# A four-layer transformer block on one core: the MLP's input rows transposed by VectorE instead of TensorE, with an exchange of quarters through DRAM

## The chip, the cores and the metric

The kernel runs on one core of a Trainium2 chip. The metric is the device time of one execution in microseconds; the median of the runs is what counts. Profiles come from one execution, and times in them run from the start of its span.

## The reference

Two attention layers and two MLP layers alternate on x of shape 1 x 2048 x 640 in float32. Both attention layers share their weights, and so do both MLPs.

```python
x = A_x
x = x + _A_ref(_layernorm(x), A_wqkv, A_wo)             # 32 heads of 20, softmax
x = x + _B_ref(_layernorm(x), B_w1, B_b1, B_w2, B_b2)   # 640 -> 1536, relu squared, 1536 -> 640
x = x + _A_ref(_layernorm(x), A_wqkv, A_wo)
x = x + _B_ref(_layernorm(x), B_w1, B_b1, B_w2, B_b2)

def _B_ref(x, w1, b1, w2, b2):
    h = jnp.einsum("bsd,df->bsf", x, w1) + b1
    r = jnp.where(h > 0, h, 0)
    return jnp.einsum("bsf,fd->bsd", r * r, w2) + b2
```

## The kernel before, in words

Rows are handled in blocks of 512 (`QB`), four to a layer (`NQB`), each of four row tiles of 128 x 640. Matrix products are made of three: every operand is split into a high part in a shorter float format (`hi`, fp32r) and the rest (`lo`), and hi x lo, lo x hi and hi x hi are accumulated (`THREE`). The split operands of the MLP are `xnT` (five tiles of 128 x 2 x 512, the normalised rows with features on the partitions) and `h`.

A layer runs `qkv`, `attention`, and then the part around the change:

- `add_heads(qb, ...)` multiplies the heads by `wo`: for each of four row tiles two chains of 15 matmuls, each followed by an add on VectorE into the row tile `x` and one call of `side()`; then the tile is stored to DRAM (`d_x`). It runs for all four blocks, one after the other. After each of the first three blocks four tiles of `w1` (512 KB each) are loaded, after the last one the remaining three and then all sixteen tiles of `w2` (480 KB each): nineteen loads in a row.
- `mlp(qb, ...)` runs for the four blocks: six chains of 15 matmuls with `w1` (one for each f; ScalarE makes relu, VectorE squares it, ScalarE makes the high part of h and VectorE the low part, in this order for each f), then eight chains of 18 matmuls with `w2`, each followed by an add on VectorE into the residual row; then the same again for the second half of F. After f = 1 to 4 of the first half the block's residual rows are loaded from `d_x` and GpSimd adds the bias `b2`. `side()` is called after each f and each w2 chain.

`side()` pops one entry from a list `steps`. That list is how the work for the next block gets its place in each engine's order: each engine executes its instructions, and SP issues its transfers, in the order in which the Python code calls them. Transfers on SP carry one of eight completion semaphores in turn; a transfer is issued only after the one eight places earlier has landed. `xtile` takes from a pool of eleven 128 x 640 tiles (`NX`), in which row tiles, residual rows and the relu results `r` share space; `slot` takes from 42 larger ones.

Before the change, `normal_rows` (a generator of nine steps) loads the next block's four row tiles, takes their statistics on VectorE (`stats`, with the inverse root on GpSimd), and normalises them on VectorE. In `mlp` its first step comes at the seventh `side()`, after the first w2 chain. Then `transposed` makes twenty 128 x 128 transposes on TensorE into five PSUM banks, and ScalarE and VectorE split each bank into high and low part over 512 columns. It is called once before the first block of the MLP, and inside blocks 0 to 2 after the third w2 chain of the second half (`(1, 0, 2)`).

Of the kernel before, what the change touches and what calls it, by code (L numbers as in the profile page):

```python
# [8 lines left out]
F32 = mybir.dt.float32  # L9
F32R = mybir.dt.float32r  # L10
AF = mybir.ActivationFunctionType
ALU = mybir.AluOpType
# [4 lines left out]
P = 128  # L17
S = 2048
D = 640
# [3 lines left out]
KD = D // P  # L23
NF = F // P
QB = 512
NQB = S // QB
# [13 lines left out]
def tile_layers(  # L40
# [11 lines left out]
    nc = tc.nc  # L52
# [6 lines left out]
    dram = ctx.enter_context(tc.tile_pool(name="dram", bufs=1, space=DRAM))  # L59
# [3 lines left out]
    def name(p):  # L63
        n_alloc[0] += 1
        return f"{p}{n_alloc[0]}"

    def slot(shape, dtype, label):
        return arena.tile(shape, dtype, tag="slot", name=name(label))

    def dma(eng, dst, src):  # L70

        if dst.dtype == F32R:
            dst = dst.bitcast(F32)
        if src.dtype == F32R:
            src = src.bitcast(F32)
        eng.dma_start(dst, src)

    def xtile(label):
        return xpool.tile([P, D], F32, tag="x", name=name(label))
# [30 lines left out]
    ps_all = Ring(0, 1, 2, 3, 4, 5, 6, 7)  # L110

    ident = cpool.tile([P, P], F32, name="ident")
# [105 lines left out]
    def at_2(f, hw, hf):  # L218

        return (((f // 6) * 2 + hf) * 6 + f % 6) * 2 + hw  # L220
# [26 lines left out]
    d_m = dram.tile([2, P, 2, 32], F32R, name="d_m")  # L247
    d_s = dram.tile([NBLK, 4, QB], F32, name="d_s")
    d_r = dram.tile([NBLK, 4, QB], F32, name="d_r")
    d_x = [dram.tile([S, D], F32, name=f"d_x{i}") for i in range(3)]  # L250

    def stats(x):

        st = small.tile([P, 2, 6], F32, tag="bst", bufs=3, name=name("bst"))
        mv = small.tile([P, 2], F32, tag="mv", bufs=6, name=name("mv"))
        for i in range(2):
            nc.vector.bn_stats(st[:, i, :], x[:, i * HALF : (i + 1) * HALF])  # L257
        nc.vector.bn_aggr(mv, st)
        var = mv[:, 1:2]
        nc.gpsimd.tensor_tensor(var, var, eps_t, op=ALU.add)  # L260
        nc.gpsimd.tensor_tensor(var, var, half_t, op=ALU.pow)
        return mv

    def normalise(eng, x, mv):
        eng.tensor_scalar(x, x, mv[:, 0:1], mv[:, 1:2], op0=ALU.subtract, op1=ALU.mult)  # L265

    def split_to(dst_hi, dst_lo, src):

        nc.scalar.copy(dst_hi, src)  # L269
        nc.vector.tensor_sub(dst_lo, src, dst_hi.bitcast(F32))  # L270

    def split_on_pool(dst_hi, dst_lo, src, r=None):

        if r is None:
            r = xtile("r")[:, :QB]
        nc.scalar.copy(r, src)
        pool_hi(dst_hi, r)
        pool_lo(dst_lo, r, dst_hi.bitcast(F32))
# [3 lines left out]

    def pool_lo(dst, a, b):
        nc.gpsimd.tensor_sub(dst, a, b)  # L284

    THREE = ((0, 0), (0, 1), (1, 0))

    def row_tile(src, r):
        t = xtile("x")
        dma(nc.sync, t, src[r * P : (r + 1) * P, :])  # L290
        return t
# [4 lines left out]
    def chain(dst, pairs):  # L296
        last = len(pairs) - 1
        for n, (a, b) in enumerate(pairs):
            nc.tensor.matmul(dst, a, b, start=(n == 0), stop=(n == last))  # L299
# [732 lines left out]
    def heads(q, qb, k):  # L1032

        ot = slot([P, 2, QB], F32R, "ot")
        dma(q, ot.rearrange("p l t -> p (l t)"), d_o[k * P : (k + 1) * P, qb])
        ready.setdefault(qb, {})[k] = ot
# [17 lines left out]
                side()  # L1054
            dma(nc.sync, x_mid[(qb * 4 + i) * P : (qb * 4 + i + 1) * P, :], x)

    def normal_rows(qb, x_src, res):

        xs = [row_tile(x_src, qb * 4 + i) for i in range(4)]
        yield  # L1060
        mvs = []
        for x in xs:
            mvs.append(stats(x))
            yield
        for x, mv in zip(xs, mvs):
            normalise(nc.vector, x, mv)
            yield
        res.extend(xs)

    def transposed(xs):  # L1070
        xnt = []
        for k in range(KD):
            dst = ps_all("xt")
            for i in range(4):
                nc.tensor.transpose(  # L1075
                    dst[:, i * P : (i + 1) * P], xs[i][:, k * P : (k + 1) * P], ident
                )
            t = slot([P, 2, QB], F32R, "xnT")
            split_to(t[:, 0, :], t[:, 1, :], dst)
            xnt.append(t)  # L1080
        return xnt

    def mlp(qb, xnt, x_mid, x_dst, side, nxt):

        xs, res = [], None
        for fh in range(2):
            hs = []
            for f in range(fh * 6, fh * 6 + 6):
                dst = ps_all("pu")
                chain(dst, [  # L1090
                    (w_1.piece(f * 10 + hw * KD + k), xnt[k][:, hx, :])
                    for k in range(KD)
                    for hw, hx in THREE
                ])
                if qb == NQB - 1:
                    w_1.past(f * 10 + 9)
                r = xtile("r")[:, :QB]
                nc.scalar.activation(r, dst, AF.Relu, bias=b1_t[:, f : f + 1])  # L1098
                nc.vector.tensor_mul(r, r, r)  # L1099
                h = slot([P, 2, QB], F32R, "h")  # L1100
                split_to(h[:, 0, :], h[:, 1, :], r)
                hs.append(h)
                if fh == 0 and f in (1, 2, 3, 4):
                    x = row_tile(x_mid, qb * 4 + f - 1)
                    nc.gpsimd.tensor_add(x, x, b2_t)
                    xs.append(x)
                side()
            for hf in range(2):
                c = slice(hf * HALF, (hf + 1) * HALF)
                for i in range(4):  # L1110
                    dst = ps_all("y")
                    chain(dst[:, :HALF], [
                        (hs[f % 6][:, hx, i * P : (i + 1) * P], w_2.piece(at_2(f, hw, hf)))
                        for f in range(fh * 6, fh * 6 + 6)
                        for hx, hw in THREE
                    ])
                    x = xs[i]
                    nc.vector.tensor_add(x[:, c], dst[:, :HALF], x[:, c])  # L1118
                    if fh == 1 and hf == 1:
                        r0 = (qb * 4 + i) * P  # L1120
                        dma(nc.sync, x_dst[r0 : r0 + P, :], x)
                    side()
                    if (fh, hf, i) == (1, 0, 2) and nxt:
                        res = transposed(nxt)
            if fh == 0 and qb == NQB - 1:
                w_2.past(at_2(5, 1, 1))
        return res

    def layer(first, x_a, x_m, x_e, front_0, ahead):
        qkv(first, x_a, front_0)  # L1130
        if first:
            dma(nc.sync, b1_t, b1.rearrange("(f p) -> p f", p=P))
            dma(nc.sync, b2_t, b2.partition_broadcast(P))
        xs = []
        attention(first, x_a, xs)
        steps = []
        for i in sorted(split):
            steps += [split.pop(i), None]
        steps += [lambda: heads(nc.scalar, NQB - 1, KD - 1)]
        for k in range(KD - 1):  # L1140
            heads(nc.sync, NQB - 1, k)

        def side():
            if steps:
                (steps.pop(0) or (lambda: None))()

        def all_steps():
            while steps:
                side()

        for qb in range(NQB):
            if qb + 1 == NQB:
                rows = []
                norm = normal_rows(0, x_m, rows)
                steps.extend([lambda: next(norm, None)] * 10)
            add_heads(qb, x_a, x_m, xs, side)
            for s in range(qb * 4, min(qb * 4 + 4, w_1.n)):
                w_1.load(s)
            if qb > 1:
                all_steps()  # L1160
        w_o.drop()
        xnt = transposed(rows)
        for s in range(w_2.n):
            w_2.load(s)
        for qb in range(NQB):
            rows = []
            if qb + 1 < NQB:
                norm = normal_rows(qb + 1, x_m, rows)
                steps.extend([None] * 6 + [lambda norm=norm: next(norm, None)] * 10)
            elif ahead:  # L1170
                some = lambda: [next(ahead, None) for _ in range(2)]
                steps.extend([None] * 7 + [some] * 21)
            xnt = mlp(qb, xnt, x_m, x_e, side, rows if qb + 1 < NQB else None)
            if qb + 1 < NQB:
                all_steps()
        steps.clear()
        w_1.drop()
        w_2.drop()
# [33 lines left out]
    for h in range(4):  # L1212
        r = 32 * h + DH
# [32 lines left out]
```

## Time and profile before

| | before |
|---|---|
| median of 3 runs | 3727.01 us (3724.64 to 3731.82) |
| profiled execution | 3726.99 us, span 3724.3 us |
| mean granted TensorE clock | 0.996 |
| TensorE matmuls | 3684.9 us busy (99%), 23572 |
| VectorE, ScalarE, GpSimd busy | 2790.1, 2553.6, 829.2 us |
| transposes at L1075 | 160, 19.9 us busy |

PE is TensorE's matmuls and PEld its weight loads, DVE is VectorE, ACT is ScalarE, POOL is GpSimd, SPq the queue from which most transfers are issued. In a timeline a row gives the start, the length, the engine, the line, the operation, output and input tiles with their shapes, the count of merged instructions, and in brackets how long the engine stood idle before it and what ended that. In a group's row the numbers behind the bar are busy time and mean duration in ns of one instruction.

### The profile page before, as it was taken

To read this page: it belongs to the slowest core of one execution; us is meant where nothing else is said; L and a number is where in the kernel's file an instruction comes from. 1 tells how busy PE (TensorE), PEld (TensorE's weight loads), DVE (VectorE), ACT (ScalarE), POOL (GpSimd) and SP (SyncE) were. 2 spreads that over 40 slices of the span, in tenths; PEclk is the share of its full clock that TensorE was granted. 3 is DMA by queue.
4 is the path that set the end of the run, shared out by engine and by line. 5 is a ranking of instruction groups with operands and counts; after the bars stand their busy time and mean duration, and the time that the engine had idled before them with its cause. 6 is when DMAs were issued, how large, how long until landed. Compare 5 with 4: busy or idle time off the path is not lost.

```text
span 3724.3 us, 64225 instructions
## 1 busy us (share of the span) xinstructions
PE 3684.9 (99%) x23572; PEld 2111.4 (57%) x23572; DVE 2790.1 (75%) x4796; ACT 2553.6 (69%) x4888; POOL 829.2 (22%) x921
## 2 busy tenths in 40 slices
PE   7999999999999999999999999999999999999999
PEld 5677343433444336999876763434434334368998
DVE  7788999999999992444567889999999999814443
ACT  2454999999999995122224459999999999941211
POOL 6430234322112211111153201121121121201110
PEclk9999999999999999999999999999999999999999
DMA  7564454432211125511255533222222111364111
GB/s 230 183 211 139 121 165 144 133 108 74 59 53 51 45 89 194 228 43 43 96 194 174 176 122 87 70 73 56 75 76 57 46 49 49 103 215 189 43 47 39
DMA packets 257682, 404.88 MB, mean 109 GB/s; under 512 B 67708, under 2 KB 114556, under 8 KB 257368
## 3 DMA queue, kind: packets, MB, share of 16 engines
q1 hardware_dynamic: 256824, 399.08, 34.1%
q8 instruction: 186, 3.05, 0.3%
q10 hardware_dynamic: 544, 1.71, 0.2%
q14 instruction: 128, 1.05, 0.1%
HBM read 263.84 MB, written 136.81 MB: 108 GB/s over the span
## 4 chain that ended last, share of the span: by engine, by line
PE 95%; DVE 3%; ACT 1%; DMA 1%; POOL 0%; issue 0%; SPq 0%; ACTq 0%; DVEq 0%; POOLq 0%
PE banks L604 27%; PE banks L299 20%; PE banks L592 20%; PE banks L495 16%; PE banks L310 7%; PE banks L357 4%; DVE mx L516 1%; PE banks L1075 0%; PE banks L387 0%; DVE bst L257 0%; DVE h L270 0%; DVE r L1099 0%; ACT h L269 0%; DVE x L265 0%; ACT r L1098 0%
## 5 line engine op out<-in xcount | busy, mean ns | idle before, releaser
L599 ACT ACTIVATE e<-banks 128x512 f32<-128x512 f32 x4096 | 2114.3, 604 | 64.0 <-PE banks L592 4.7
L507 DVE TENSOR_REDUCE mx<-banks 128x1 f32<-128x512 f32 x2940 | 1845.9, 683 | 189.9 <-PE banks L495 116.3
L495 PE MATMUL banks<-k,q 60*128 60x512 f32 x3744 | 1155.7, 436 | 6.3 <-DVE mx L516 2.3
L592 PE MATMUL banks<-q,k 62*128 62x512 f32 x4096 | 1152.7, 435 | 2.1 <-DVE mx L516 1.7
L604 PE MATMUL banks<-e,vg 128*32 128x512 f32 x8192 | 1093.8, 605 | 0.0
L592 PEld LDWEIGHTS banks<-q,k 62*128 62x128 f32 x4096 | 601.1, 185 | 701.1 <-ACT e L599 665.9
L495 PEld LDWEIGHTS banks<-k,q 60*128 60x128 f32 x3744 | 538.1, 185 | 332.1 <-DVE mx L507 206.0
L604 PEld LDWEIGHTS banks<-e,vg 128*32 128x32 f32 x8192 | 161.6, 108 | 357.9 <-issue 330.9
L527 ACT ACTIVATE rl<-banks 128x512 f32<-128x512 f32 x352 | 191.3, 596 | 248.0 <-PE banks L495 247.9
L299 PE MATMUL banks<-w,h 128*128 128x320 f32 x2304 | 351.1, 311 | 2.7 <-DVE h L270 2.5
L299 PEld LDWEIGHTS banks<-w,h 128*128 128x128 f32 x2304 | 339.4, 188 | 11.7 <-DVE h L270 6.4
L299 PE MATMUL banks<-xnT,w 128*128 128x512 f32 x1440 | 331.6, 391 | 0.0
L310 PE MATMUL banks<-xnT,wqk 128*128 128x512 f32 x1200 | 320.5, 410 | 3.7 <-POOL wqk L284 2.5
L537 DVE CUSTOM_DVE_ANT_0 rl<-banks,rl 128x512 f32<-128x512 f32 x352 | 229.1, 688 | 112.3 <-PE banks L495 103.3
L1098 ACT ACTIVATE r<-banks,b_t 128x512 f32<-128x512 f32 x96 | 66.1, 688 | 356.3 <-PE banks L299 352.5
L299 PEld LDWEIGHTS banks<-xnT,w 128*128 128x128 f32 x1440 | 270.7, 189 | 55.7
L516 DVE TENSOR_REDUCE mx<-banks 128x2 f32<-128x1024 f32 x226 | 271.7, 1220 | 16.1 <-PE banks L495 15.1
L310 PEld LDWEIGHTS banks<-xnT,wqk 128*128 128x128 f32 x1200 | 217.8, 191 | 88.3 <-issue 42.7
L648 POOL TENSOR_TENSOR few<-few,minus_t 128x16 f32<-128x16 f32 x62 | 179.8, 2900 | 286.1 <-DMA few<-d_s 285.9
L659 POOL TENSOR_TENSOR o<-o 128x512 f32<-128x512 f32 x62 | 79.5, 1283 | 612.7 <-DMA o<-d_r 376.9
L1118 DVE TENSOR_TENSOR x<-banks,x 128x320 f32<-128x320 f32 x128 | 62.9, 491 | 196.2 <-PE banks L299 187.0
L281 POOL CAST mr<-nt 128x32 fp32r<-128x32 f32 x64 | 13.4, 210 | 808.6 <-DVE nt L563 775.1
(76 smaller groups left out, 1986.6 us busy)
## 6 DMA issues: line engine op xcount, KB each, us to landing
q<-d_qk SPq DMA_DIRECT2D x744, 80.0 KB
d_qk<-ev SPq DMA_DIRECT2D x80, 512.0 KB
k<-d_qk SPq DMA_DIRECT2D x468, 80.0 KB
x<-d_x SPq DMA_DIRECT2D x96, 320.0 KB
d_o<-ot SPq DMA_DIRECT2D x248, 80.0 KB
ot<-d_o SPq DMA_DIRECT2D x38, 512.0 KB
d_v<-v SPq DMA_DIRECT2D x32, 512.0 KB
vg<-d_v SPq DMA_DIRECT2D x32, 512.0 KB
```

The costliest lines, as they stand in the source:

```text
L299: nc.tensor.matmul(dst, a, b, start=(n == 0), stop=(n == last))
L310: nc.tensor.matmul(dst, w_qk.piece(pos * 10 + hw * KD + k), xt_[tb][k][:, hx, :], start=(n == 0), stop=(n == 3 * KD - 1),)
L357: nc.tensor.matmul(dst[:, :HALF], xt_[tb][k][:, hx, i * P : (i + 1) * P], w_v.piece(k * 4 + hw * 2 + hf), start=(j == 0), stop=(j == 3 * K ...
L495: nc.tensor.matmul(dst, q_t[t][b : b + 60, p, sub * P : (sub + 1) * P], k_t[t // NQB, c][b : b + 60, p, :], start=True, stop=True,)
L507: nc.vector.tensor_reduce(maxima(t)[:, 2 * p + par, sub, c : c + 1], dst, axis=AX.X, op=ALU.max)
L516: nc.vector.tensor_reduce(maxima(t)[:, 2 * p : 2 * p + 2, sub, c], dst, axis=AX.X, op=ALU.max)
L527: nc.scalar.activation(res[par], dst[:, par, :], AF.Relu)
L537: nc.vector.tensor_tensor_reduce(out=r[par], in0=dst[:, par, :], in1=r[par], scale=1.0, scalar=LEAST, op0=ALU.add, op1=ALU.max, accum_out= ...
L592: nc.tensor.matmul(dst, k_t[t // NQB, kt // 4][b : b + 62, p, (kt % 4) * P : (kt % 4 + 1) * P], q_t[t][b : b + 62, p, :], start=True, stop ...
L599: nc.scalar.activation(es[p][:, par, :], dst, AF.Exp, scale=SCALE)
L604: nc.tensor.matmul(acc[32 * h : 32 * h + 32, :], v_t[t // NQB, kt // 8][:, kt % 8, 32 * h : 32 * h + 32], es[p][:, par, :], start=(kt == 0 ...
L648: nc.gpsimd.tensor_tensor(few, few, minus_t, op=ALU.pow)
```

## The change

A row tile is now transposed in three moves. `turn` subtracts the mean and scales on VectorE, writing with the four 32-column groups of each 128 features moved apart, transposes all 32 x 32 blocks of the 128 x 640 tile with one VectorE instruction, and stores it to a DRAM scratch tile `d_t`. `turn_load` reads it back with four transfers, one for each group of 32 partitions, in pieces of 640 bytes; this completes the 128 x 128 transposes. `parts` then splits each 128 x 128 piece: ScalarE makes the high part, GpSimd (k = 0, 2, 4) or VectorE (k = 1, 3) the low part, twenty of each for a block instead of five wider ones.

The order changes too. The first block's rows are stepped in `add_heads` from block 2 on rather than in block 3, and their parts are made in the last four side calls of block 3, so that nothing is left between the last `wo` chain and the first `w1` chain. In `mlp` the first five `side()` calls (after f = 0 to 4 of the first half) now load the next block's rows and take the statistics, one is left out, then follow four turns and four loads after the w2 chains. The parts are made after the first w2 chain of the second half, `(1, 0, 0)`. TensorE's part of this work is gone.

```diff
+    d_t = dram.tile([4, P, D], F32, name="d_t")
...
+    def turn(x, mv, i):
+        y = xtile("y")
+        nc.vector.tensor_scalar(
+            y.rearrange("p (c k i) -> p k c i", c=4, k=KD),
+            x.rearrange("p (k c i) -> p k c i", c=4, k=KD),
+            mv[:, 0:1], mv[:, 1:2], op0=ALU.subtract, op1=ALU.mult,
+        )
+        nc.vector.transpose(x, y)
+        dma(nc.sync, d_t[i], x)
+        return y
+
+    def turn_load(y, i):
+        src = d_t[i].rearrange("(a j) (c r) -> c j a r", a=4, c=4)
+        for c in range(4):
+            dma(nc.sync, y[32 * c : 32 * c + 32].rearrange("j (a r) -> j a r", a=4), src[c])
+
+    def parts(res, i, y):
+        view = y.rearrange("p (a k i) -> p k a i", a=4, k=KD)
+        for k, t in enumerate(res):
+            hi, lo = (
+                t[:, h, i * P : (i + 1) * P].rearrange("p (a i) -> p a i", a=4) for h in range(2)
+            )
+            nc.scalar.copy(hi, view[:, k])
+            (nc.vector if k % 2 else nc.gpsimd).tensor_sub(lo, view[:, k], hi.bitcast(F32))
+
+    def turned_rows(qb, x_src, ys):
+        xs = [row_tile(x_src, qb * 4 + i) for i in range(4)]
+        yield
+        mvs = []
+        for x in xs:
+            mvs.append(stats(x))
+            yield
+        for i, mv in enumerate(mvs):
+            ys.append(turn(xs[i], mv, i))
+            xs[i] = x = None
+            yield
+        for i, y in enumerate(ys):
+            turn_load(y, i)
+            yield
...
-                    if (fh, hf, i) == (1, 0, 2) and nxt:
-                        res = transposed(nxt)
+                    if (fh, hf, i) == (1, 0, 0) and nxt:
+                        res = new_rows()
+                        for j in range(4):
+                            parts(res, j, nxt.pop(0))
...
-            if qb + 1 == NQB:
-                rows = []
-                norm = normal_rows(0, x_m, rows)
-                steps.extend([lambda: next(norm, None)] * 10)
+            if qb + 2 == NQB:
+                rows, xnt = [], []
+                norm = turned_rows(0, x_m, rows)
+                steps.extend([lambda: next(norm, None)] * 11 + [
+                    lambda: (xnt.extend(new_rows()), next(norm, None)),
+                    lambda: (parts(xnt, 0, rows[0]), parts(xnt, 1, rows[1]), next(norm, None)),
+                    lambda: parts(xnt, 2, rows[2]),
+                    lambda: parts(xnt, 3, rows[3]),
+                    rows.clear,
+                ])
             add_heads(qb, x_a, x_m, xs, side)
...
-            if qb > 1:
+            if qb + 1 == NQB:
                 all_steps()
         w_o.drop()
-        xnt = transposed(rows)
         for s in range(w_2.n):
             w_2.load(s)
...
             if qb + 1 < NQB:
-                norm = normal_rows(qb + 1, x_m, rows)
-                steps.extend([None] * 6 + [lambda norm=norm: next(norm, None)] * 10)
+                norm = turned_rows(qb + 1, x_m, rows)
+                step = lambda norm=norm: next(norm, None)
+                steps.extend([step] * 5 + [None] + [step] * 8)
```

More of the change, by code (lines that the diff above doesn't have):

```diff
@@ L284, in pool_lo, with new_rows @@
         nc.gpsimd.tensor_sub(dst, a, b)
+    def turn(x, mv, i):
[34 more added lines that the diff above has]
+            yield
+    def new_rows():
+        return [slot([P, 2, QB], F32R, "xnT") for _ in range(KD)]
     THREE = ((0, 0), (0, 1), (1, 0))
@@ L1055, in add_heads @@
             dma(nc.sync, x_mid[(qb * 4 + i) * P : (qb * 4 + i + 1) * P, :], x)
[L1057 to L1081, printed above, removed]
     def mlp(qb, xnt, x_mid, x_dst, side, nxt):
```

## The prediction

> **What bounds the kernel now.** I read the page first (engine shares and the chain that ended last), then TensorE's timeline around the first layer's hand-over from attention to the MLP, then SP's, VectorE's and GpSimd's timelines of the same stretch.
>
> ```profile
> PE 3684.9 (99%) x23572; PEld 2111.4 (57%) x23572; DVE 2790.1 (75%) x4796; ACT 2553.6 (69%) x4888; POOL 829.2 (22%) x921
> PE 95%; DVE 3%; ACT 1%; DMA 1%; POOL 0%; issue 0%; SPq 0%; ACTq 0%; DVEq 0%; POOLq 0%
> ```
>
> TensorE is busy 99% of the span and carries 95% of the chain. Any time taken from TensorE is gained, and any wait put in front of it is paid in full. TensorE's timeline (start, length, group, idle before it):
>
> ```profile
> 1479.74 41.67 PE L299 MATMUL banks<-wo,ot 128*128 128x320 f32 x283
> 1521.25 0.42 PE L1075 MATMUL banks<-ident,x 128*128 128x128 f32 x2
> 1522.52 0.33 PE L1075 MATMUL banks<-ident,x 128*128 128x128 f32 x1 [0.85 <-DVE x L265]
> 1523.04 2.08 PE L1075 MATMUL banks<-ident,x 128*128 128x128 f32 x17 [0.19 <-DVE x L265]
> 1524.87 20.70 PE L299 MATMUL banks<-xnT,w 128*128 128x512 f32 x90
> 1545.40 2.88 PE L299 MATMUL banks<-w,h 128*128 128x320 f32 x17
> 1548.45 18.89 PE L299 MATMUL banks<-w,h 128*128 128x320 f32 x127 [0.17 <-DVE h L270]
> ...
> 1596.25 2.35 PE L1075 MATMUL banks<-ident,x 128*128 128x128 f32 x20
> 1598.35 13.45 PE L299 MATMUL banks<-w,h 128*128 128x320 f32 x90
> ```
>
> The MLP runs almost without a gap: the six w1 chains (20.70 us, 3.45 each), one 0.17 us wait for the last h, the eight w2 chains (18.89 us for the last seven, 2.7 each). The transposes cost 3.62 us ahead of block 0 (1521.25 to 1524.87) and 2.10 us inside each of three blocks (1596.25 to 1598.35). Per layer that is 3.62 + 3 x 2.10 = 9.9 us, 20 us for both: all that the change can win.
>
> **SP's queue and what waits on it.** The end of add_heads and the start of the MLP are where transfers are dense:
>
> ```profile
> 1487.14 1.90 SPq L76 DMA_DIRECT2D w<-d_w  x4
> ...
> 1504.80 1.84 SPq L76 DMA_DIRECT2D w<-d_w  x4
> 1507.00 1.95 SPq L76 DMA_DIRECT2D x<-d_x  x4
> 1509.06 13.23 SPq L76 DMA_DIRECT2D d_x<-x  x4
> 1522.34 17.60 SPq L76 DMA_DIRECT2D w<-d_w  x19
> 1540.76 8.80 SPq L76 DMA_DIRECT2D x<-d_x  x8
> ...
> 1612.80 13.58 SPq L76 DMA_DIRECT2D x<-d_x  x8
> ```
> ```profile
> 1514.14 0.89 DVE L257 BATCH_NORM_STATS2 bst<-x 128x6 f32<-128x320 f32 x2 [5.40 <-DMA x<-d_x]
> 1515.06 0.21 DVE L258 BATCH_NORM_AGGREGATE mv<-bst 128x2 f32<-128x12 f32 x1
> 1515.18 0.47 DVE L1053 TENSOR_TENSOR x<-banks,x 128x320 f32<-128x320 f32 x1
> 1516.61 0.44 DVE L1053 TENSOR_TENSOR x<-banks,x 128x320 f32<-128x320 f32 x1
> ...
> 1529.33 0.69 DVE L1099 TENSOR_TENSOR r<-r 128x512 f32<-128x512 f32 x1 [2.18 <-ACT r L1098]
> 1530.70 0.69 DVE L270 TENSOR_TENSOR h<-r,h 128x512 fp32r<-128x512 f32 x1 [0.69 <-ACT h L269]
> ...
> 1534.10 0.69 DVE L270 TENSOR_TENSOR h<-r,h 128x512 fp32r<-128x512 f32 x1 [0.69 <-ACT h L269]
> ...
> 1547.70 0.69 DVE L270 TENSOR_TENSOR h<-r,h 128x512 fp32r<-128x512 f32 x1 [0.69 <-ACT h L269]
> ...
> 1616.04 2.09 DVE L1099 TENSOR_TENSOR r<-r 128x512 f32<-128x512 f32 x1 [3.72 <-ACT r L1098]
> 1618.82 1.29 DVE L270 TENSOR_TENSOR h<-r,h 128x512 fp32r<-128x512 f32 x1 [0.69 <-ACT h L269]
> ```
> ```profile
> 1550.13 6.16 POOL L1105 TENSOR_TENSOR x<-x,b_t 128x640 f32<-128x640 f32 x4 [29.74 <-DMA x<-d_x]
> ...
> 1616.02 7.49 POOL L1105 TENSOR_TENSOR x<-x,b_t 128x640 f32<-128x640 f32 x4 [54.14 <-DMA x<-d_x]
> ```
> ```profile
> 1525.00:1545.00 20.00, 20.00 (x91) 16.52 (x90) 9.06 (x14) 7.54 (x13) 0.00 (x0) 1.00 1.02 406
> 26.00:29.00 3.00, 2.68 (x9) 2.19 (x10) 0.95 (x2) 0.59 (x1) 1.11 (x1) 0.50 1.00 320
> ```
>
> Nineteen weight loads start at 1522.34, fill the DMA engines (share 1.02 and 406 GB/s in the window 1525 to 1545), and the first x tile behind them is usable at 1550.13: 27.8 us after the first weight load was issued. GpSimd waits for it, and before the change nobody minds, because the statistics come after the first w2 chains. With a free queue an x tile takes 3.2 us (1612.80 to 1616.02).
>
> **The change, block 0 (the deciding part).** turned_rows is now stepped at the first five side() calls of mlp, not from the seventh on. So in block 0 the four row loads of block 1 stand on SP directly behind the nineteen weight loads, ahead of the residual rows, and the first bn_stats stands on VectorE behind the second h and ahead of the third r*r. VectorE executes in order. The second h ends at 1534.79, 9.9 us after the w1 chains begin at T (1524.87 before). The row cannot be there: the weight loads stand behind the last d_x store, that waits for the last add of add_heads, and this add now stands behind the last parts on VectorE, about 1 us after T. The row is there at T + 1 + 27.8 = T + 28.8, and VectorE idles some 19 us. Behind it wait r*r and the low half of h for f = 2 to 5, and behind those ScalarE's cast of h. TensorE finishes its six w1 chains (eight banks hold them) and stands at the third h of the first w2 chain.
>
> What VectorE then has to do: four statistics of 1.1 us (1514.14 to 1515.18, and its overlap), four times r*r, cast, low half at 2.06 us (1529.33 to 1531.39), 4 x 1.1 + 4 x 2.06 = 12.6 us. GpSimd's four bias adds now fall into this: where it ran them beside VectorE, r*r took 2.09 instead of 0.69 us and the low half 1.29 instead of 0.69; three such operations at 0.9 us give 2.7 us. The last h is at T + 44.1; before it was at 1548.39, T + 23.5. **Cost 20.6 us a layer**, from 17 (no contention, stores sooner) to 24 (every operation slowed).
>
> The clock: after an idle stretch in the first 26 us the granted clock was 0.50 for 3 us (window 26 to 29). After a 20 us gap the same should follow: 3 to 6 us at half speed lose 1.5 to 3 us; I take 2, range 0 to 3.5. [...]
>
> **The first block's own rows.** The removed 3.62 us is replaced by a wait for the exchange. The row loads now follow the weight loads of 1487.14. In the trace weight loads at 1504.80 and rows behind them gave the first statistic at 1514.14, 9.3 us later; one more x tile stands ahead now (0.8 us at 406 GB/s), so 1497.3. Four statistic-and-add pairs at 1.4 us (1515.18 to 1516.61) end at 1503. A turn is a subtract-and-scale, a transpose and an add:
>
> ```profile
> L265 DVE TENSOR_SCALAR x<-x,mv 128x640 f32<-128x640 f32 x64 | 40.9, 654 | 1.7 <-POOL mv L261 1.7
> L563 DVE STREAM_TRANSPOSE nt<-nm 128x32 f32<-128x32 f32 x64 | 13.6, 212 | 6.3
> L258 DVE BATCH_NORM_AGGREGATE mv<-bst 128x2 f32<-128x12 f32 x64 | 13.4, 209 | 2.2
> L284 POOL TENSOR_TENSOR w<-raw,w 128x128 fp32r<-128x128 f32 x6 | 2.8, 461 | 0.2
> L173 ACT CAST wqk<-raw 128x128 fp32r<-128x128 f32 x2 | 0.6, 312 | 0.0
> SPq L76 <- DMA w<-d_w: 16.6, 19, 2.0
> ```
>
> The 128x640 transpose is not in the trace. From below it is one pass like L265, 0.65 us; from above twenty 32-column ones, 20 x 0.212 = 4.2 us. The 32-column one takes no longer than a 12-element aggregate (209 ns), so its time is mostly fixed and I take 0.8. [...]
>
> Four turns of 1.85 us end at 1510.5; the eleven x tiles are all in use then, so two of them wait for a store to land, some 1.5 us each: 1513.5. The fourth store stands behind the four weight loads at the end of add_heads(2), 2 MB or 5.2 us at 406 GB/s, and lands at about 1520.5. SP issues a transfer only when the eighth before it has landed (the 19 waits of the last row are that), and each turn_load is four transfers; the last four go out about 1524.5 and land 2.3 us later. One cast (312 ns) and one low part (461 ns) on, T is 1527.7: **2.8 us later than before**. From below: transfers that overtake the weight loads hide the exchange and T is 1522 (-2.9); from above, the 4.2 us transpose or slow 640-byte pieces add 5 (+8). A half clock at T costs nothing, since TensorE then waits for h in any case.
>
> **Inside blocks 0 to 2** the transposes go: -6.3 us. The exchange and parts are covered. turn takes about 1.95 us with its add, of 2.7 us per w2 chain; each turn_load has eight chains' time; twenty casts (6.2 us) and twelve GpSimd parts (5.5 us) lie in the seven chains (18.9 us) before the next block, and VectorE's adds behind its eight parts have eight banks of cover. In blocks 1 and 2 rows land in 3 us, ahead of their statistic; but 1.1 us of statistics now stands beside 2.06 us of h work in a 3.45 us chain, with the bias adds spread over it. It just fits without contention and is some 1.3 us late with it: **+2.6 us for two blocks**, range 0 to 6.
>
> **Sum per layer**: 20.6 + 2 + 2.8 - 6.3 + 2.6 = 21.7; layer 2 has the same order, so 43 us. The profiled execution took 3726.99 us (span 3724.3), the median is 3727.01: **3770 us**.
>
> **The rivals.** *The row comes in time* (a win): the loads are not served in the order of issue, or the weight loads clear sooner. The point is T + 11.6: VectorE can lose 1.7 us and still have the last h in time. Then 2 x (-6.3) with T from -2.9 to +2.8 gives 3709 to 3720, say 3714. For it: the trace shows the order of service at two places only, and the last weight load could be done sooner with fewer stores beside it. Against it: x behind 19 weight loads was usable only 9.4 us after its own issue (1540.76 to 1550.13). *The exchange decides* (worse): the first block waits for a slow transpose or small packets as well, T + 5 more in each layer, 3780 to 3792; it counts from a transpose over 2 us on. *Half of it*: no contention, early T, no clock loss, 2 x (17 - 2.9 - 6.3) = 16, 3743. The changed program holds no transpose of these rows on TensorE, so it does do what it says.
>
> **How the numbers follow.** Forecast 0.78, worse exchange 0.08, half of it 0.06, row in time 0.06, the strip between 0.02. The range runs from the half case, 3743, to the worse one, 3792; 0.08 lies below and a little above. A measurement here tells about 0.2%, 7.5 us: faster 0.06, same 0.02, slower 0.92.
>
> **What would show it.** Right: VectorE idle some 19 us ahead of one bn_stats per layer, released by x<-d_x; TensorE idle about 20 us in the first w2 chain of each layer, ended by h; the granted clock below 1 after it; 160 fewer transposes. Wrong: bn_stats of block 1 that starts within 12 us of the first w1 chain; a w2 chain that begins 21 us after it as before; or TensorE waiting mostly for parts of xnT.

## The result and the profile after

The changed kernel takes 3790.05 us (median of 4 runs, 3789.18 to 3793.14) against 3728.12 us (4 runs of the kernel before on the same chip): ratio 1.0167, 95% interval 1.015 to 1.0185, some 62 us slower. Its profiled execution has a span of 3787.8 us, 63.5 us more than before, and a mean granted TensorE clock of 0.987 instead of 0.996.

The page of the kernel after, shares of the engines and of the chain that ended last:

```profile
PE 3688.4 (97%) x23412; PEld 2110.0 (56%) x23412; DVE 2842.9 (75%) x4852; ACT 2565.3 (68%) x5008; POOL 878.2 (23%) x1017
PE 89%; DVE 5%; DMA 4%; ACT 1%; SPq 1%; issue 1%; POOL 1%; ACTq 0%; DVEq 0%; POOLq 0%
```

TensorE has 160 matmuls fewer (the transposes are gone) and yet is busy 3.5 us longer: some of what is left ran at a granted clock of 0.50 (windows in the last section). In the chain that ended last, TensorE has lost 6 points, most of them to transfers (1% to 4%) and to VectorE (3% to 5%): the time is now in waits. TensorE's timeline of the first layer shows where (start, length, group, idle before it and what ended it):

```profile
1450.10 68.76 PE L348 MATMUL banks<-wo,ot 128*128 128x320 f32 x465
1528.36 23.43 PE L348 MATMUL banks<-xnT,w 128*128 128x512 f32 x90 [9.50 <-ACT xnT L313]
1551.63 1.04 PE L348 MATMUL banks<-w,h 128*128 128x320 f32 x6
1560.61 1.36 PE L348 MATMUL banks<-w,h 128*128 128x320 f32 x3 [7.94 <-ACT h L270]
...
1574.19 21.22 PE L348 MATMUL banks<-w,h 128*128 128x320 f32 x129 [1.61 <-ACT h L270]
1595.25 20.59 PE L348 MATMUL banks<-xnT,w 128*128 128x512 f32 x90
...
1637.51 20.59 PE L348 MATMUL banks<-xnT,w 128*128 128x512 f32 x90
1657.93 2.34 PE L348 MATMUL banks<-w,h 128*128 128x320 f32 x14
1661.80 0.42 PE L348 MATMUL banks<-w,h 128*128 128x320 f32 x1 [1.52 <-DVE h L271]
1664.04 20.72 PE L348 MATMUL banks<-w,h 128*128 128x320 f32 x129 [1.83 <-ACT h L270]
1684.60 20.59 PE L348 MATMUL banks<-xnT,w 128*128 128x512 f32 x90
```

Three places wait. Ahead of the first w1 chain 9.50 us for a part of xnT, where before 3.62 us went to the transposes. In block 0's first w2 chain, from 1551.63 to 1574.19, TensorE runs 15 matmuls in 22.56 us and otherwise waits for h. In block 1 it waits twice more for h, 1.52 and 1.83 us. The second halves are clean and shorter: 1595.25 to 1637.51 is 42.26 us, where before the stretch with the transposes (1567.18 to 1611.63) took 44.45.

Such differences, taken from the starts of the same groups in both traces, add up to 63.9 us; the last block of the kernel is 0.4 us shorter, which makes the 63.5 us of the span (us, after less before):

| stretch | layer 1 | layer 2 | both |
|---|---|---|---|
| start of the last `wo` group to the first w1 chain | +6.0 | +4.5 | +10.6 |
| block 0, first half | +24.6 | +23.0 | +47.6 |
| blocks 0 to 2, second halves (transposes gone) | -6.6 | -6.6 | -13.1 |
| block 1, first half | +4.8 | +4.3 | +9.2 |
| block 2, first half | +6.2 | +4.2 | +10.3 |
| what lies ahead of these (attention; for layer 2 also block 3 of layer 1) | -2.5 | +1.9 | -0.7 |
| sum | | | +63.9 |

VectorE's timeline of the same stretch shows what block 0 waited for:

```profile
1540.67 0.69 DVE L271 TENSOR_TENSOR h<-r,h 128x512 fp32r<-128x512 f32 x1 [0.69 <-ACT h L270]
1558.22 0.89 DVE L258 BATCH_NORM_STATS2 bst<-x 128x6 f32<-128x320 f32 x2 [16.85 <-DMA x<-d_x]
...
1562.23 1.47 DVE L1122 TENSOR_TENSOR r<-r 128x512 f32<-128x512 f32 x1
1564.39 2.05 DVE L271 TENSOR_TENSOR h<-r,h 128x512 fp32r<-128x512 f32 x1 [0.68 <-ACT h L270]
...
1567.40 1.76 DVE L1122 TENSOR_TENSOR r<-r 128x512 f32<-128x512 f32 x1
1569.85 2.04 DVE L271 TENSOR_TENSOR h<-r,h 128x512 fp32r<-128x512 f32 x1 [0.68 <-ACT h L270]
...
1650.99 2.07 DVE L271 TENSOR_TENSOR h<-r,h 128x512 fp32r<-128x512 f32 x1 [0.69 <-ACT h L270]
```

After the second h, VectorE stands 16.85 us for a row of block 1 (1541.36 to 1558.22); r * r and the low half of h for four values of f wait behind it. Four of these operations then take two to three times their 0.69 us, and the same happens in block 1 at 1650.99. GpSimd's timeline has the neighbour, the bias add into a residual row, and in block 1 what stands ahead of it:

```profile
1561.63 1.53 POOL L1128 TENSOR_TENSOR x<-x,b_t 128x640 f32<-128x640 f32 x1 [31.86 <-DVE h L271]
...
1649.82 0.53 POOL L261 TENSOR_TENSOR mv<-mv,eps_t 128x1 f32<-128x1 f32 x1 [1.67 <-DVE mv L259]
1650.43 0.55 POOL L262 TENSOR_TENSOR mv<-mv,half_t 128x1 f32<-128x1 f32 x1
1650.94 1.57 POOL L1128 TENSOR_TENSOR x<-x,b_t 128x640 f32<-128x640 f32 x1
```

The early statistics also decide when the bias adds run. Before, the four adds of block 1 ran one behind the other (7.49 us from 1616.02). Now the inverse root of a statistic (L261 and L262) stands ahead of the next add, and three of the four adds start so just as VectorE comes to a low half of h (1650.94 and 1650.99); the first starts when its row lands, also beside a low half. These four low halves take 2.01 to 2.07 us.

The queue on SP, with start and length of each group of issues:

```profile
1510.78 1.83 SPq L76 DMA_DIRECT2D w<-d_w  x4
1512.70 0.40 SPq L76 DMA_DIRECT2D d_t<-x  x1
...
1523.92 1.93 SPq L76 DMA_DIRECT2D y<-d_t  x4
...
1530.32 16.87 SPq L76 DMA_DIRECT2D w<-d_w  x19
1548.05 9.72 SPq L76 DMA_DIRECT2D x<-d_x  x8
```

The last turned tile is stored right behind four w1 loads, and the sixteen quarter loads are issued in order, the last four from 1523.92 to 1525.85, 7 us after the last `wo` matmul (1518.86). Block 1's rows are issued behind nineteen weight loads: 1530.32 to the first statistic at 1558.22 is 27.9 us.

### The profile page after: what moved, and what is told of

Same layout as the page of the kernel before. It is cut to its first block, busy times and chain, and to the rows that moved or that the text cites. A ratio compares the mean times of both kernels' runs of the same rounds, so it can differ in the third digit from the quotient of the medians.

```text
span 3787.8 us, 64610 instructions
## 1 busy us (share of the span) xinstructions
PE 3688.4 (97%) x23412; PEld 2110.0 (56%) x23412; DVE 2842.9 (75%) x4852; ACT 2565.3 (68%) x5008; POOL 878.2 (23%) x1017
## 4 chain that ended last, share of the span: by engine, by line
PE 89%; DVE 5%; DMA 4%; ACT 1%; SPq 1%; issue 1%; POOL 1%; ACTq 0%; DVEq 0%; POOLq 0%
PE banks L653 27%; PE banks L641 19%; PE banks L348 17%; PE banks L544 15%; PE banks L359 6%; PE banks L406 4%; DVE h L271 1%; DMA x<-d_x 1%; DVE bst L258 1%; DVE r L1122 1%; DMA w<-d_w 1%; SPq L76 1%; ACT h L270 1%; DVE mx L565 1%; DMA d_t<-x 1%
## 5 line engine op out<-in xcount | busy, mean ns | idle before, releaser
L348 PE MATMUL banks<-w,h 128*128 128x320 f32 x2304 | 367.2, 319 | 47.6 <-ACT h L270 36.3
L348 PEld LDWEIGHTS banks<-w,h 128*128 128x128 f32 x2304 | 351.4, 194 | 62.0 <-ACT h L270 42.6
```

## The experiments

Each kernel was timed against the kernel before on its own chip. Four shared one chip (before: 3724.9 us, 15 runs), the other three another (3725.06 us, 10 runs). What a run gains or loses is counted here against its own before, since the medians of before differ by some 3 us (3728.12 us beside the changed kernel).

**Statistics after the w2 chains (stats_late).** The changed kernel, with the rows and statistics of the next block put back to where they stood before the change:

```diff
-                steps.extend([step] * 5 + [None] + [step] * 8)
+                steps.extend([None] * 6 + [step] * 13)
```

> The change kept whole, but in mlp the thirteen steps of turned_rows start at the seventh side call, after the first w2 chain, where the rows and statistics stood before. Theory A (the place of the rows and statistics costs the time, not the way of transposing): the last-h waits of blocks 0 to 2 go, some 25 us in block 0 and 2 to 4.5 us in blocks 1 and 2 of each layer; what is left is the first block's wait, 5.9 and 4.4 us longer than the transposes it replaced, against 6.3 us won per layer inside the blocks: 3728 + 10.3 - 12.6 = 3726 us. Theory B (the exchange through DRAM, the VectorE transposes and the small parts cost it): most of the 62 us stays, 3770 us or more.

Measured 3731.61 us, ratio 1.0018 (1.0009 to 1.0027). One line takes away 55 of the 62 us: 6.7 are left. TensorE's timeline in layer 1:

```profile
1529.26 22.77 PE L348 MATMUL banks<-xnT,w 128*128 128x512 f32 x90 [10.80 <-ACT xnT L313]
...
1554.97 18.89 PE L348 MATMUL banks<-w,h 128*128 128x320 f32 x127 [0.17 <-DVE h L271]
```

Block 0's first w2 chains are back to a 0.17 us wait. What is left is the first block's exchange, 10.80 us of wait, and w1 chains that take 22.77 us instead of 20.70 behind it.

**The order alone (order_only).** The kernel before, transposes on TensorE, with only its rows and statistics moved to the early places (its normalising moves up with them, to the first w2 chains):

```diff
-                steps.extend([None] * 6 + [lambda norm=norm: next(norm, None)] * 10)
+                steps.extend([lambda norm=norm: next(norm, None)] * 5 + [None] + [lambda norm=norm: next(norm, None)] * 5)
```

> The kernel before, with TensorE's transposes as they were; only the steps of normal_rows in mlp are put where the change has them, the first five at the first five side calls. Theory A: TensorE starts the w1 chains at the usual time, the row lands 25.3 us after that, the last h of block 0 comes some 20 us late and the clock costs 2 more, blocks 1 and 2 lose 2 to 4.5 us each: 3728 + 2 x (21.5 + 6.6) = 3784 us. Theory B: no change, 3728 us.

Measured 3783.57 us, ratio 1.0155 (1.0141 to 1.0168): 59 us of loss without any turn, exchange or part. TensorE shows the same pattern as after:

```profile
1553.09 1.36 PE L299 MATMUL banks<-w,h 128*128 128x320 f32 x3 [6.17 <-ACT h L269]
...
1566.66 21.08 PE L299 MATMUL banks<-w,h 128*128 128x320 f32 x129 [1.61 <-ACT h L269]
```

So the loss belongs to the place of the rows and statistics, not to who transposes. The two experiments frame it from both sides: the order costs 55 to 59 us, everything else in the change together 3 to 7.

**Block 1's rows ahead of the weights (rows_ahead).** The early statistics stay, but in each MLP block 1's row loads are issued before the w2 loads:

```diff
+        ahead_rows = []
+        ahead_norm = turned_rows(1, x_m, ahead_rows)
+        next(ahead_norm)
         for s in range(w_2.n):
             w_2.load(s)
...
-                norm = turned_rows(qb + 1, x_m, rows)
+                norm = turned_rows(qb + 1, x_m, rows) if qb else ahead_norm
+                rows = rows if qb else ahead_rows
...
-                steps.extend([step] * 5 + [None] + [step] * 8)
+                steps.extend([step if qb else None] + [step] * 4 + [None] + [step] * 8)
```

> The change kept whole, but the four row loads of block 1 are issued ahead of the sixteen w2 loads (behind the three w1 loads); the statistics stay where the change put them on VectorE. Theory A with the queue as the cause: rows land about 8 us after the w1 chains begin, before VectorE comes to the statistics, and block 0 loses nothing or up to 4 us; 3790 - 2 x 23 = 3744 us. If the statistics as such overload VectorE in block 0, whenever the rows land: 3780 us or more.

Measured 3745.71 us, ratio 1.0057 (1.0043 to 1.0071): 41 of the 62 us come back although the statistics still stand between the f's. VectorE and then TensorE:

```profile
1543.08 0.88 DVE L258 BATCH_NORM_STATS2 bst<-x 128x6 f32<-128x320 f32 x2
```
```profile
1556.82 18.89 PE L348 MATMUL banks<-w,h 128*128 128x320 f32 x127 [0.17 <-DVE h L271]
...
1642.11 0.41 PE L348 MATMUL banks<-w,h 128*128 128x320 f32 x1 [1.53 <-DVE h L271]
```

The first statistic starts without a wait, and block 0 runs clean: its loss began with the row behind the nineteen weight loads. (The residual rows still stand behind the weights here, and VectorE waits until 1565.45 for the first of block 0's bias adds, when its last low half of h, 0.69 us from 1556.07, is long done; so the adds don't meet VectorE's work on h.) Block 1 still waits at 1642.11, so that has another cause.

**No bias adds (no_bias).** The changed kernel without GpSimd's adds of b2 (they are left out of the sum):

```diff
                     x = row_tile(x_mid, qb * 4 + f - 1)
-                    nc.gpsimd.tensor_add(x, x, b2_t)
                     xs.append(x)
```

> The change kept whole, but GpSimd's add of b2 to the residual rows is left out, so the output lacks that bias. Theory A with GpSimd beside VectorE as the cause in blocks 1 and 2: without the bias adds the statistics (1.1 us) and h (2.06 us) fit the 3.45 us chain, blocks 1 and 2 lose nothing any more (some 18 us in both layers), and block 0's last h comes 4 us sooner per layer: 3790 - 26 = 3764 us. If the statistics alone are too much for VectorE between the chains: 3782 us or more.

Measured 3763.02 us, ratio 1.0099 (1.0084 to 1.0114): 27 us less than after, or 24 with each against its own before. TensorE, and VectorE in block 1:

```profile
1572.31 21.74 PE L348 MATMUL banks<-w,h 128*128 128x320 f32 x129 [1.61 <-ACT h L270]
...
1659.69 18.89 PE L348 MATMUL banks<-w,h 128*128 128x320 f32 x127 [0.17 <-DVE h L271]
```
```profile
1648.68 0.69 DVE L271 TENSOR_TENSOR h<-r,h 128x512 fp32r<-128x512 f32 x1 [0.69 <-ACT h L270]
```

Block 1 is back to 0.17 us. In block 0 the last wait ends 40.8 us after the start of the first w1 chain (1531.47 in this run) instead of 45.8: the bias adds cost nearly 5 us there as well (the row was 0.3 us sooner in this run). The first half of block 0 is 4.5 and 4.4 us shorter than after's in the two layers; with the 19.5 us of blocks 1 and 2 in the table that is 28.4 us, against 26.7 between the spans of the two profiled executions.

**The first block by TensorE again (hybrid).** stats_late, and the first block of each MLP with the old rows and transposes; blocks 1 to 3 keep VectorE's:

```diff
-            if qb + 2 == NQB:
-                rows, xnt = [], []
-                norm = turned_rows(0, x_m, rows)
...
+            if qb + 1 == NQB:
+                rows = []
+                norm = normal_rows(0, x_m, rows)
+                steps.extend([lambda: next(norm, None)] * 10)
...
+        xnt = transposed(rows)
```

> As stats_late, but the first block of each MLP is transposed by TensorE as before the change, with its rows in add_heads of block 3; only blocks 1 to 3 use VectorE and the exchange. Theory A: no term of loss is left, and three times 2.10 us per layer are won: 3728 - 12.6 = 3715 us. Theory B: the exchange still costs in blocks 0 to 2, 3740 us or more.

Measured 3711.45 us, ratio 0.9963 (0.995 to 0.9977), 13.5 us faster than before; the table's second halves gave 13.1. Turn, exchange and parts of blocks 1 to 3 are hidden in full, and the transposes that they replace are gained: in its trace the first halves of blocks 0 to 2 last as long as before within 0.1 us, the second halves 2.2 us less each.

**w1 out of the exchange's way (w1_later).** stats_late, and the four w1 loads after `add_heads(2)` moved behind `add_heads(3)`:

```diff
-            for s in range(qb * 4, min(qb * 4 + 4, w_1.n)):
-                w_1.load(s)
+            if qb + 2 != NQB:
+                for s in range(qb * 4 - 4 * (qb + 1 == NQB), min(qb * 4 + 4, w_1.n)):
+                    w_1.load(s)
```

> stats_late, and the four w1 loads that stood between add_heads of blocks 2 and 3 are issued after block 3, with the other three. Theory C (the first block waits because the exchange stands behind 2 MB of weights): TensorE's wait ahead of the first w1 chain falls from 10.8 to some 5 us per layer, time 3731 - 11 = 3720 us. If the wait is VectorE's turns or the sixteen quarter loads on SP alone: 3728 us or more.

Measured 3715.14 us, ratio 0.9971 (0.9959 to 0.9982). The wait ahead of the first w1 chain falls from 10.80 to 3.94 us in layer 1 (8.64 to 3.65 in layer 2), 11.9 of the some 16.5 us gained on stats_late; between the two traces about 3 more fall into the attention, which the edit doesn't touch, and were not followed up. SP's waits show the cause: from 1511 to 1526 it stood 4.1 us for w1 loads to land in after's trace, and in w1_later's no weight load is issued there before 1525.11. TensorE:

```profile
1523.15 23.13 PE L348 MATMUL banks<-xnT,w 128*128 128x512 f32 x90 [3.94 <-ACT xnT L313]
```

**Quarter loads on two queues (two_queues).** w1_later, and half of the first block's quarter loads issued from ScalarE's queue:

```diff
-            dma(nc.sync, y[32 * c : 32 * c + 32].rearrange("j (a r) -> j a r", a=4), src[c])
+            dma(nc.scalar if two and c % 2 else nc.sync, y[32 * c : 32 * c + 32].rearrange("j (a r) -> j a r", a=4), src[c])
```

> w1_later, and of the first block's quarter loads two of each four are issued by ScalarE, which is idle there, not by SP. Theory D (what is left of the first block's wait is SP's issue time, 16 loads at 0.4 us): 2 to 3 us less per layer than w1_later, 3715 us. If the wait is the landing of the last store and load: the same as w1_later.

Measured 3706.72 us, ratio 0.9949 (0.9936 to 0.9961): faster than both kernels, and 8.4 us less than w1_later where 4 to 6 were expected. The median is also below the hybrid's, but the intervals of the two ratios overlap. TensorE in both layers:

```profile
1522.71 21.00 PE L348 MATMUL banks<-xnT,w 128*128 128x512 f32 x90 [2.14 <-ACT xnT L313]
...
3362.01 21.01 PE L348 MATMUL banks<-xnT,w 128*128 128x512 f32 x90 [1.38 <-ACT xnT L313]
```

The wait falls by 1.8 us in layer 1 (2.3 in layer 2), and in layer 1 the w1 chains take 21.00 instead of 23.13 us. That second gain had not been counted. (Another 2.6 us between the two traces lie ahead of the exchange, which this edit doesn't touch.) Windows around the start of the w1 chains, w1_later's first and then two_queues'. A row has the window, its length, the busy time of TensorE, its weight loads, VectorE, ScalarE and GpSimd, each with its count, and then the granted clock, the DMA engines' share and GB/s:

```profile
1522.00:1526.00 4.00, 2.85 (x7) 2.13 (x8) 1.37 (x4) 1.09 (x5) 1.39 (x3) 0.50 0.31 118
```
```profile
1522.00:1526.00 4.00, 3.25 (x13) 2.48 (x14) 1.86 (x5) 1.10 (x5) 1.84 (x4) 1.00 0.47 166
```

After 3.94 us of idling the clock is 0.50, after 2.14 us it is 1.00. From the start of the last `wo` group to the end of block 0's first half, two_queues is 0.9 us shorter than before in layer 1 and 1.8 us in layer 2: there the exchange costs less than the transposes that it replaces.

## Why the prediction came out as it did

The direction and its cause were right, and the time lay inside the range, 20 us above the forecast of 3770. That it stayed inside is partly luck: it lies 2 us below the upper end, 3792, which stood there for a slower exchange, and most of the missing time came from another step, blocks 1 and 2. By its steps (T is the start of the first w1 chain):

- **Block 0, the row that cannot be there: right.** Forecast T + 28.8, measured T + 29.9 (1558.22 less 1528.36); forecast idling 19 us, measured 16.85, because the second h came later, the w1 chains running at half clock. TensorE's waits in the first w2 chain add up to 17.1 us, forecast about 20. order_only and rows_ahead show that the place of the row loads behind the weight loads is what starts block 0's loss.
- **Contention in block 0: too small.** The 2.7 us of the sum were worked out from three operations at 0.9 us more. Taking the bias adds away gave nearly 5 us. With the clock, block 0 cost 24.6 and 23.0 us against 22.6.
- **The clock: right.** 2 us forecast; in layer 1 the 129 matmuls from 1574.19 took 21.22 us where 127 take 18.89, so 2.0 us over. The half clock lasted some 4 us from there and nearly 6 us behind the 9.50 us wait (0.50 from 1528.36 to about 1534), both within the forecast's 3 to 6 us. That a half clock at T costs nothing held in this kernel, where block 0 waits for the row anyway. It stops holding once the statistics are late: stats_late pays 2.1 us (22.77 against 20.70, the clock 0.50 in the window 1526 to 1530 and 0.56 from 1530 to 1534).
- **The first block's exchange: mis-sized, 10.6 us for both layers against 5.6.** The turns came out right in sum: the fourth transpose ends at 1511.21, forecast 1513.5, and the `wo` chains came 2.5 us earlier in this run. A turn took 2.1 us (1507.31 to 1509.40) instead of 1.85, with one wait for a landing store instead of two. The step that failed is "the last four go out about 1524.5 and land 2.3 us later". They go out one after the other from 1523.92 to 1525.85; measured from the end of the `wo` chains, the first of them is some 2 us later than forecast and the last some 4, and T is 3 us later. w1_later and two_queues show the two parts: the four w1 loads on SP, and the issue of sixteen loads by one engine (the last four took 1.93 us).
- **Blocks 1 and 2: mis-sized, the main error.** "It just fits without contention and is some 1.3 us late with it" gave 2.6 us a layer, range 0 to 6; 11.0 and 8.5 were measured, outside that range, 14 of the 20 us missed. Two things were left out. First, the early statistics bring a bias add to the low half of h for four values of f, and beside the add, 1.54 to 1.57 us long, that low half takes longer: in block 1 2.01 to 2.07 us instead of 0.69 four times, 5.4 us more in all. VectorE's round for one f takes 4.36 us with its statistic, where a w1 chain takes 3.45. Second, after two short waits in a row (1.52 and 1.83 us) the clock was 0.50 in the window 1664 to 1667, and the 129 matmuls from 1664.04 took 20.72 instead of 19.2 us (18.89 for 127).
- **The transposes' gain inside the blocks: right.** -6.3 a layer forecast, -6.6 measured, and hybrid isolates it.
- **The price of the transpose: right.** Taken at 0.8 us between 0.65 and 4.2, it is 0.845 us in after's groups by line, and the strided scale ahead of it 0.93 instead of the 0.65 us assumed:

```profile
L291 DVE TENSOR_SCALAR y<-x,mv 128x640 f32<-128x640 f32 x32 | 29.8, 930 | 3.9 <-DMA d_t<-x 3.9
L296 DVE STREAM_TRANSPOSE x<-y 128x640 f32<-128x640 f32 x32 | 27.1, 845 | 1.1
```

The rival in which the exchange decides was counted from a transpose over 2 us on and did not come about, although the time fell inside its 3780 to 3792. The rival in which the row comes in time was wrong for this order, and rows_ahead is that rival made true for block 0.

## What to carry to other kernels

An instruction that waits for a transfer, put into an in-order engine's stream ahead of work that the bottleneck needs, hands that transfer's whole queue to the bottleneck (VectorE's 16.85 us for a row behind nineteen weight loads, 17.1 us of waits on TensorE): ask what stands before the load on its queue, not how long the load takes. Work that just fits beside a chain is priced with its neighbours on other engines (here a low half of 2.07 instead of 0.69 us), and with the clock that a short wait can cost (here 0.50 after 1.52 and 1.83 us). When a change bundles a new method with a new order, try each alone: here the method gained 0.5% once the statistics were late, the four w1 loads stood behind its exchange and half of the quarter loads had a second queue, and the order alone lost 1.6%.

## What the runs showed of the hardware that was not expected

- The low half of h on VectorE (128x512, inputs r and h) took about as long as the rest of the GpSimd add of 128x640 beside it and its own time together: 2.07 us from 1650.99, while the bias add ran from 1650.94 to 1652.51, so the 1.52 us left of it plus 0.69 make 2.2, within some 0.15 us. In no_bias, without the add, it took 0.69 us. What holds it up beside the add was not shown.
- The granted clock fell to 0.50 without one long gap. In block 1 of after two waits of 1.52 and 1.83 us with 0.42 us of work between were enough:

```profile
1661.00:1664.00 3.00, 0.42 (x1) 0.19 (x1) 2.30 (x5) 0.62 (x1) 1.25 (x3) 0.97 0.00 0
1664.00:1667.00 3.00, 2.96 (x10) 2.74 (x11) 2.15 (x4) 0.00 (x0) 0.01 (x1) 0.50 0.02 5
1667.00:1670.00 3.00, 3.00 (x22) 3.00 (x21) 1.71 (x3) 0.00 (x0) 0.00 (x0) 0.96 0.28 109
```

A single wait of 2.14 us left it at 1.00, but the length of one wait doesn't decide alone: in w1_later the clock fell an estimated 2.2 us into the wait (TensorE idle from 1519.21, clock 0.91 in the window 1519 to 1522 and 0.50 from 1522 to 1526), in after an estimated 5 us into it (idle from 1518.86, 1.00 in the window 1519 to 1522, 0.81 from 1522 to 1525, 0.50 from 1525 to 1528.3). What decides it was not shown.
